# Sums by accumulating transfers, a deeper matrix scheme in two more chunks, and another bank in the last step of a normalised attention with four experts

## The chip, the cores and the metric

The kernel runs on one core of a Trainium2 chip. The metric is the device time of one execution, in microseconds (us). The kernel before took 1731.64 us, the median of three runs (1731.56 to 1731.66). The engines are TensorE (PE), VectorE (DVE), ScalarE (ACT), GpSimd (POOL) and SyncE (SP); PE writes to PSUM banks, and POOL and SP issue transfers. PEld in the profile is the weight load of TensorE.

## The reference

Attention without softmax over 8 batches, 8 heads, 576 positions and a head size of 64, then four experts on the 4608 tokens, each 512 to 1024 to 512 with a ReLU between, mixed by probabilities:

```python
kv = einsum('bhsd,bhse->bhde', k, v)
out = einsum('bhsd,bhde->bhse', q, kv)
x = out / sqrt(mean(out * out, axis=-1) + 1e-06) * g_norm      # then (B,H,S,D) -> (B*S, H*D)
p = domain_probs / (domain_probs.sum(-1, keepdims=True) + 1e-09)
for e in range(4):
    h = maximum(x @ w1[e], 0.0)
    out += p[:, e:e+1] * (h @ w2[e])
```

All is float32.

## The kernel before

The tokens are nine chunks of 512, so that experts and chunks make 36 steps, s = 9e + c, from 0 to 35. Each step has an up product (`x @ w1`) and a down product (`h @ w2`). Both are done by a Strassen-Winograd scheme, which replaces the eight products of a matrix in quarters by seven, at the price of more additions. The up product does it on two levels: seven outer products, and each of those made of seven inner ones.

```python
ORDER = (1, 6, 2, 5, 7, 4, 3)      # inner products, in this order
MERGED = (1, 6, 5, 7, 4, 3, 2)
OUTER = (1, 2, 6, 5, 3, 7, 4)      # outer products, in this order
BANKS = {"u1": 2, "u2": 2, "db": 2, "ab": 2}      # the eight PSUM banks
```

After each outer product m of the up product, whose 128 x 1024 result lies in a tile `made[m]` ("big"), the outer sums that have become possible are made. `add` is one tensor_tensor of 128 x 1024 on DVE or POOL, `relu` one activation of 128 x 1024 in place on ACT, `unit(f)` a new tile:

```python
for i, m in enumerate(OUTER):
    ...                      # 49 matmul groups in all; ACT and DVE empty the banks
    if m == 2:
        add(key, unit(1), made[1], made[2])
        relu(key, h[1])
    elif m == 6:
        add(key, made[1], made[1], made[6])
    elif m == 5:
        add(key, made[6], made[1], made[5])
    elif m == 3:
        add(key, unit(21), made[6], made[3])
        relu(key, h[21])
        add(key, unit(7), h[1], h[21], ALU.subtract)
    elif m == 7:
        ...                  # made[1] += made[7], then h[4], h[5], h[6]
    elif m == 4:
        add(key, unit(2), made[1], made[4])
        relu(key, h[2])
        add(key, unit(3), h[2], h[6], ALU.subtract)
```

The down product has two forms. `down` has one level: seven products for each of two halves of the tokens, each of four matmuls with 256 columns. `down_deep` has two levels: 49 products, each of two matmuls with 128 columns; it needs quarter sums of h and of w2, and outer sums of the results.

```python
def down(s, e, c):                            # one level
    for t in range(2):
        for j, m in enumerate(MERGED):
            kind = "ab" if e and t else "db"
            if m == 1:
                banks[1] = Buf(kind, f"d1_{s}_{t}")
            elif m in (2, 5):
                banks[2] = Buf(kind, f"d{m}_{s}_{t}")
            for kt in range(4):
                nc.tensor.matmul(ps[:, 0:256], ...)           # L1095
            ...                                               # weighted into acc: ACT or DVE
def down_deep(s, e, c):                       # two levels
    for i, group in enumerate(((1, 6), (7, 5), (4, 2), (3,))):
        ...                  # quarter sums of h: one add of 512 and two of 256 columns for each m
        for j, mm in enumerate(ORDER):
            for o, m in enumerate(group):
                for kt in range(2):
                    nc.tensor.matmul(ps[:, o * P:(o + 1) * P], ...)      # L1170
        ...                  # five copies on ACT and two sums on DVE for each group;
                             # seven outer sums of 128 x 512 in all (L1236), then weighted into acc

if e and c < NCH - 1:        # NCH is 9
    down_deep(s, e, c)
else:
    down(s, e, c)
```

So the nine steps of the first expert and the last step of each later expert (17, 26, 35) have the plain form. Results go to DRAM: in later experts by accumulating transfers that POOL issues, in the last step by plain stores of SP.

```python
if e and not again:          # again: s == 35
    nc.gpsimd.dma_start(out=dst, in_=cell(i)[parts, :], accum_op=ALU.add)      # L1065
else:
    nc.sync.dma_start(out=dst, in_=cell(i)[parts, :])                          # L1067
```

The order of all instructions on each engine is fixed ahead of the run by a list scheduler inside the kernel (`Plan.layout`). It simulates the engines with assumed durations, takes for each engine the most urgent operation that is ready, gives out buffers, and fixes what it took as that engine's order. For a transfer that POOL issues it assumes that it has landed 5.5 us after its issue, which takes 1.0 us:

```python
op.end = busy[eng] = t + op.cost[eng]
if op.kb:
    op.end += 5.5
```

On the chip each engine follows that order, and waits wherever an operand isn't there yet.

Of the kernel before, what the change touches and what calls it, by code (L numbers as in the profile page):

```python
# [10 lines left out]
ALU = mybir.AluOpType  # L11
# [219 lines left out]
def kernel(  # L231
# [36 lines left out]
    nc = tc.nc  # L268

    B, H, S, D = q.shape  # L270
    E, DM, F = moe_w1.shape
# [5 lines left out]
    NCH = B + 1  # L277
# [56 lines left out]
    plan = Plan()  # L334
# [4 lines left out]
    def dve(n):  # L339
        return {"DVE": 0.155 + 0.00104 * n}  # L340

    def act(n):
        return {"ACT": 0.155 + 0.00088 * n}
# [507 lines left out]
    def up(s, e, views):  # L851
        made = {}
        h = {}

        def add(key, to, a, b, op=ALU.add, where=either):
            combine(
                key, where(2 * NT), lambda: to.ap[:], lambda: a.ap[:], lambda: b.ap[:], op,
                [a, b], [to],
            )

        def relu(key, b):
            plan.add(
                key, act(2 * NT),
                lambda eng: nc.scalar.activation(out=b.ap[:], in_=b.ap[:], func=ACT.Relu),  # L864
                reads=[b], writes=[b],
            )

        for i, m in enumerate(OUTER):
            n = f"{s}_{m}"
            whole = made[m] = Buf("big", f"m{n}")  # L870
            bank = {
                1: Buf("u1", f"u1_{n}"), 2: Buf("u2", f"u2_{n}"), 5: Buf("u2", f"u3_{n}"),
            }
            snap = {}
            for j, mm in enumerate(ORDER):
                key = s + (i + j / 7) / 7
                ps = bank[{2: 2, 5: 5, 3: 5}.get(mm, 1)]

                def product(eng, m=m, mm=mm, ps=ps):
                    for u in range(2):  # L880
                        nc.tensor.matmul(  # L881
                            ps.ap[:, u * P:(u + 1) * P],
                            lhsT=w1f[e][m][mm][1]()[:, u * P:(u + 1) * P], rhs=views[m][mm][1](),
                            start=(mm in (1, 5) and u == 0), stop=True, skip_group_check=True,
                        )

                op = plan.add(
                    key, pe(2, P), product,
                    reads=w1f[e][m][mm][0] + [views[m][mm][0]] + ([ps] if mm == 2 else []),
                    **{"parts" if mm == 2 else "writes": [ps]},  # L890
                    after=last[-2:-1] if mm == 1 else seeds if mm == 5 else (),
                )
                op.marks, op.seed = (ps, HN), mm == 2
                if mm == 3:
                    last.append(op)

                def copy(to, where, ps=ps, key=key):
                    return plan.add(
                        key - 0.4, act(HN),
                        lambda eng: nc.scalar.activation(  # L900
                            out=where(), in_=ps.ap[:, 0:HN], func=ACT.Copy),
                        reads=[ps], parts=[to],
                    )

                def total(a, t, src, add_, whole=whole, key=key):
                    plan.add(
                        key - 0.4, dve(HN),
                        lambda eng: nc.vector.tensor_tensor(  # L908
                            out=block(whole, a, t), in0=src.ap[:, 0:HN], in1=add_.ap[:], op=ALU.add),
                        reads=[src, add_], parts=[whole],  # L910
                    )

                if mm == 1:
                    seeds = [copy(bank[2], lambda b=bank[2]: b.ap[:, 0:HN])]
                elif mm in (6, 7):
                    snap[mm] = Buf("snap", f"s{mm}_{n}")
                    copy(snap[mm], lambda b=snap[mm]: b.ap[:])
                if mm == 2:
                    copy(whole, lambda whole=whole: block(whole, 0, 0))
                elif mm == 7:  # L920
                    total(1, 1, bank[5], snap[7])
                elif mm == 4:
                    copy(whole, lambda whole=whole: block(whole, 1, 0))
                elif mm == 3:
                    total(0, 1, ps, snap[6])
            key = s + (i + 1) / 7

            def unit(f):
                h[f] = Buf("big", f"h{f}_{s}")
                return h[f]  # L930

            if m == 2:
                add(key, unit(1), made[1], made[2])
                relu(key, h[1])
            elif m == 6:
                add(key, made[1], made[1], made[6])
            elif m == 5:
                add(key, made[6], made[1], made[5])
            elif m == 3:
                add(key, unit(21), made[6], made[3])  # L940
# [3 lines that stand above are left out]
                add(key, made[1], made[1], made[7])  # L944
                add(key, unit(4), made[1], made[5], where=dve)
                relu(key, h[4])
                add(key, unit(5), h[21], h[4], where=dve)
                add(key, unit(6), h[5], h[1], ALU.subtract, dve)
            elif m == 4:
                add(key, unit(2), made[1], made[4])  # L950
                relu(key, h[2])
                add(key, unit(3), h[2], h[6], ALU.subtract)
        hidden[s] = h
# [123 lines left out]
    def down(s, e, c):  # L1077
        h = hidden.pop(s)
        base = s + 1.2
        merge, send = result(s, e, c, base)  # L1080
        second = []
        for t in range(2):
            banks = {}
            for j, m in enumerate(MERGED):
                key = base + (7 * t + j + 0.5) / 14
                kind = "ab" if e and t else "db"
                if m == 1:
                    banks[1] = Buf(kind, f"d1_{s}_{t}")
                elif m in (2, 5):
                    banks[2] = Buf(kind, f"d{m}_{s}_{t}")  # L1090
                ps = banks[1 if m in (1, 6, 7, 4) else 2]

                def product(eng, m=m, t=t, ps=ps):
                    for kt in range(4):
                        nc.tensor.matmul(  # L1095
                            ps.ap[:, 0:HN], lhsT=four(h[m])[:, kt // 2, t, kt % 2, :],
                            rhs=w2f[e][m].ap[:, kt * HN:(kt + 1) * HN],
                            start=(m in (1, 2, 5) and kt == 0), stop=(kt == 3),
                            skip_group_check=True,
                        )  # L1100

                op = plan.add(
                    key, pe(4, HN), product, reads=[h[m], w2f[e][m]], writes=[ps],
                    after=second[-1:] if t and m in (1, 5) else (),
                )
                op.marks = ps, HN
                if m == 2:
                    second.append(op)
                i, half, fresh = {
                    1: (t, 0, True), 2: (t, 0, False), 6: (t, 1, True), 3: (t, 1, False),  # L1110
                    5: (2 + t, 1, True), 7: (2 + t, 1, False), 4: (2 + t, 0, True),
                }[m]
                merge(key - 0.4, [ps], lambda ps=ps: ps.ap[:, 0:HN], i, half, fresh)
            send(base + 0.5 * (t + 1), t)
            send(base + 0.5 * (t + 1), 2 + t)
# [171 lines left out]
    for e in range(E):  # L1287
        for c in range(NCH):
            s = e * NCH + c
# [11 lines left out]
                up(s, e, x_views.pop(s))  # L1301
            if c == 0 and e:
                inner[e]()
            if e and c < NCH - 1:
                if not primed:
                    banks = [Buf("ab", f"prime{i}") for i in range(2)]

                    def prime(eng, banks=banks):
                        for b in banks:
                            nc.tensor.matmul(b.ap[:, 0:P], lhsT=ident[:], rhs=ident[:], start=True,  # L1310
                                             stop=False, skip_group_check=True)
                            nc.tensor.matmul(b.ap[:, P:HN], lhsT=ident[:], rhs=ident[:], start=False,
                                             stop=True, skip_group_check=True)

                    primed.append(plan.add(s + 1.1, pe(4, P), prime, writes=banks))
                    primed[0].marks = banks[0], HN
# [3 lines that stand above are left out]
# [7 lines left out]
    with tc.manual_schedule(engines={ENG.PE, ENG.DVE, ENG.Activation, ENG.Pool, ENG.SP}):  # L1327
# [4 lines left out]
        for op in order:  # L1332
# [6 lines left out]
            made = op.fn(op.eng)  # L1339
# [34 lines left out]
```

## Time and profile before

| What | Value |
|---|---|
| time | 1731.64 us |
| span of the profiled execution | 1729.4 us |
| busy: PE, PEld, DVE, ACT, POOL | 1719.6, 1652.0, 1222.8, 938.6, 616.5 us |
| matmul records | 15334 |
| HBM read and written | 145.30 and 73.14 MB |

One float32 matmul instruction leaves two matmul records in this trace: the plain down product has 12 steps of 56 matmuls, which is 672, and its groups have 1344 records together. The recorded ends of matmuls overlap, so the time of a matmul is read from the distance of the starts and not from the mean duration of a record. A group "L360" holds the adds of a helper, through which nearly all tensor_tensor operations of DVE and POOL go, so the shapes must be kept apart.

### The profile page before, as it was taken

The numbers are of one execution on the slowest core, as the hardware profiler recorded it, in microseconds if no ns is written. First come the engines' busy times: TensorE is split into PE (matmuls) and PEld (weight loads), VectorE is DVE, ScalarE is ACT, GpSimd is POOL, SyncE is SP. The second block draws the span as 40 slices with busy tenths as digits, with TensorE's granted clock in tenths as the row PEclk, the third lists the DMA queues.
The fourth block names the chain that finished last, engine by engine and source line by source line (L and its number), as shares of the span: only waits on it lengthen the run. The fifth ranks groups of instructions, "written<-read, shape, count | busy, mean of one in ns | idle before, by whom it ended". The sixth has DMA issues, their size and how long they took to land.

```text
span 1729.4 us, 38448 instructions
## 1 busy us (share of the span) xinstructions
PE 1719.6 (99%) x15334; PEld 1652.0 (96%) x15334; DVE 1222.8 (71%) x1968; ACT 938.6 (54%) x2300; POOL 616.5 (36%) x561
## 2 busy tenths in 40 slices
PE   9999999999999999999999999999999999999998
PEld 7699999999999999999999999999999999999997
DVE  4755655565676777777788877777788877777774
ACT  3354544454444565656555556566555556665652
POOL 3421323133334333333345333333345333333331
PEclk9999999999999999999999999999999999999999
DMA  9756444633333343534465344444475344444442
GB/s 240 218 161 193 153 122 131 193 135 128 147 130 99 94 114 104 116 106 113 131 185 110 99 110 111 111 111 110 114 204 110 98 111 111 110 110 109 112 99 49
DMA packets 148596, 220.94 MB, mean 128 GB/s; under 512 B 49600, under 2 KB 90816, under 8 KB 148416
## 3 DMA queue, kind: packets, MB, share of 16 engines
q1 hardware_dynamic: 133312, 191.21, 35.6%
q0 software_dynamic: 15104, 27.27, 11.0%
q8 instruction: 120, 1.97, 0.5%
q14 instruction: 60, 0.49, 0.1%
HBM read 145.30 MB, written 73.14 MB: 126 GB/s over the span
## 4 chain that ended last, share of the span: by engine, by line
PE 99%; POOL 0%; ACT 0%; DVE 0%; issue 0%; POOLq 0%
PE u L881 45%; PE db L1170 19%; PE db L1095 15%; PE ab L1170 12%; PE ab L1095 2%; PE u L968 2%; PE ab L634 1%; PE ab L678 1%; PE ab L620 1%; PE ab L1323 1%; PE ab L660 1%; PE db L660 0%; POOL rt L551 0%; PE ab L722 0%; PE ab L704 0%; PE ab L738 0%
## 5 line engine op out<-in xcount | busy, mean ns | idle before, releaser
L360 DVE TENSOR_TENSOR big<-big,big 128x1024 f32<-128x1024 f32 (+1 forms) x449 | 440.9, 995 | 34.9 <-ACT big L864 23.8
L881 PE MATMUL u<-xf,big 128*128 128x128 f32 x3104 | 453.3, 276 | 0.0
L881 PEld LDWEIGHTS u<-xf,big 128*128 128x128 f32 x3104 | 401.5, 192 | 2.2
L881 PE MATMUL u<-xf,w1y 128*128 128x128 f32 x2652 | 389.9, 276 | 0.0
L908 DVE TENSOR_TENSOR big<-u,snap 128x256 f32<-128x256 f32 x430 | 181.3, 422 | 235.9 <-PE u L881 176.4
L881 PEld LDWEIGHTS u<-xf,w1y 128*128 128x128 f32 x2652 | 343.6, 192 | 2.1
L900 ACT ACTIVATE snap<-u 128x256 f32<-128x256 f32 x490 | 187.7, 383 | 251.6 <-PE u L881 212.2
L1095 PE MATMUL db<-big,big 128*128 128x256 f32 x1136 | 269.0, 382 | 2.1 <-DVE big L560 2.1
L1095 PEld LDWEIGHTS db<-big,big 128*128 128x128 f32 x1136 | 207.1, 192 | 25.4 <-DVE big L560 2.3
L900 ACT ACTIVATE big<-u 128x256 f32<-128x256 f32 x430 | 164.7, 383 | 110.6 <-PE u L881 75.5
L360 POOL TENSOR_TENSOR big<-big,big 128x256 f32<-128x256 f32 (+1 forms) x139 | 172.5, 1248 | 132.3 <-DVE big L360 46.8
L1170 PE MATMUL db<-big,big 128*128 128x128 f32 x1056 | 146.9, 276 | 0.4 <-ACT snap L1198 0.4
L864 ACT ACTIVATE big<-big 128x1024 f32<-128x1024 f32 x128 | 134.5, 1051 | 3.4 <-POOL big L360 2.1
L1170 PEld LDWEIGHTS db<-big,big 128*128 128x128 f32 x1056 | 132.1, 192 | 0.6 <-ACT snap L1198 0.6
L1236 POOL TENSOR_TENSOR big<-big 128x512 f32<-128x512 f32 x26 | 33.0, 1268 | 269.2 <-DVE big L360 263.9
L1198 ACT ACTIVATE snap<-db 128x256 f32<-128x256 f32 x192 | 68.4, 356 | 100.0 <-PE db L1170 95.1
L360 POOL TENSOR_TENSOR big<-big 128x512 f32<-128x512 f32 (+1 forms) x57 | 70.3, 1232 | 126.8 <-DVE big L360 102.6
L1170 PE MATMUL db<-kv,big 128*128 128x128 f32 x804 | 114.7, 275 | 0.0
L1065 POOL DMA_DIRECT2D out_dram<-big x100 | 91.2, 987 | 47.4 <-ACT snap L1198 22.8
L900 ACT ACTIVATE u<-u 128x256 f32<-128x256 f32 x245 | 90.9, 371 | 28.1 <-PE u L881 8.0
L1170 PEld LDWEIGHTS db<-kv,big 128*128 128x128 f32 x804 | 102.1, 192 | 0.1
L1206 DVE TENSOR_TENSOR big<-ab,snap 128x256 f32<-128x256 f32 x140 | 59.1, 422 | 57.4 <-ACT snap L1198 31.9
(213 smaller groups left out, 2676.9 us busy)
## 6 DMA issues: line engine op xcount, KB each, us to landing
xf<-x SPq DMA_DIRECT2D x108, 512.0 KB, 3.6
out_dram<-big POOLq DMA_DIRECT2D x84, 256.0 KB, 5.8
xf<-x_h SPq DMA_DIRECT2D x81, 256.0 KB, 3.2
xf<-x SPq DMA_DIRECT2D x81, 256.0 KB, 3.3
x<-xf SPq DMA_DIRECT2D x36, 512.0 KB, 6.1
big<-in_moe_w_dram SPq DMA_DIRECT2D x25, 512.0 KB, 4.8
small<-in_q_dram SPq DMA_DIRECT2D x72, 128.0 KB, 4.8
kv<-in_k_dram SPq DMA_DIRECT2D x30, 288.0 KB, 4.8
```

Source lines behind the costliest of these rows:

```text
L360: lambda eng: adder(eng).tensor_tensor(out=out_(), in0=a(), in1=b(), op=op),
L864: lambda eng: nc.scalar.activation(out=b.ap[:], in_=b.ap[:], func=ACT.Relu),
L881: nc.tensor.matmul(ps.ap[:, u * P:(u + 1) * P], lhsT=w1f[e][m][mm][1]()[:, u * P:(u + 1) * P], rhs=views[m][mm][1](), start=(mm in (1, 5) ...
L900: lambda eng: nc.scalar.activation(out=where(), in_=ps.ap[:, 0:HN], func=ACT.Copy),
L908: lambda eng: nc.vector.tensor_tensor(out=block(whole, a, t), in0=src.ap[:, 0:HN], in1=add_.ap[:], op=ALU.add),
L968: nc.tensor.matmul(bank.ap[:], lhsT=two(w.ap[:])[:, kt, ut * P:(ut + 1) * P], rhs=two(xh[dh].ap[:])[:, kt, :], start=(dh == kt == 0), stop ...
L1065: nc.gpsimd.dma_start(out=dst, in_=cell(i)[parts, :], accum_op=ALU.add)
L1095: nc.tensor.matmul(ps.ap[:, 0:HN], lhsT=four(h[m])[:, kt // 2, t, kt % 2, :], rhs=w2f[e][m].ap[:, kt * HN:(kt + 1) * HN], start=(m in (1, ...
L1170: nc.tensor.matmul(ps.ap[:, o * P:(o + 1) * P], lhsT=b.ap[:, col:col + P], rhs=w2q[e][m][mm][1]()[:, kt, :], start=(mm in (1, 5) and o == ...
L1198: lambda eng: nc.scalar.activation(out=where(), in_=group_of(ps.ap), func=ACT.Copy),
L1206: lambda eng: nc.vector.tensor_tensor(out=cell(tq, dq), in0=group_of(src.ap), in1=group_of(add_.ap), op=ALU.add,),
L1236: lambda eng: adder(eng).tensor_tensor(out=whole(to), in0=whole(a), in1=whole(b), op=ALU.add),
```

## The change

It has three parts. In steps 9 to 33, three of the outer sums of each up product are no longer made by DVE or POOL, but by a transfer within SBUF which adds its source onto its destination. POOL issues it (one instruction, 128 rows of 4096 bytes). That frees the arithmetic engines, and spares the new tile of the sum, as the sum lies where an operand lay. Second, the down products of steps 17 and 26 take the two-level form, so that the plain form is left to the first expert and step 35. Third, in step 35 the bank of products 2, 3, 5 is taken from "u2", which the up products no longer need there, in place of "db" and "ab".

```diff
+        by_dma = e > 0 and s < 34
+
+        def accumulate(key, to, a):
+            plan.add(
+                key, {"POOL": 1.0},
+                lambda eng: nc.gpsimd.dma_start(out=to.ap[:], in_=a.ap[:], accum_op=ALU.add),
+                reads=[a, to], writes=[to], kb=512,
+            )
...
-            if m == 2:
+            if m == 2 and by_dma:
+                h[1] = made[2]
+                accumulate(key, h[1], made[1])
+                relu(key, h[1])
+            elif m == 2:
                 add(key, unit(1), made[1], made[2])
                 relu(key, h[1])
+            elif m == 6 and by_dma:
+                accumulate(key, made[6], made[1])
+                made[1] = made[6]
+                made[6] = None
             elif m == 6:
                 add(key, made[1], made[1], made[6])
             elif m == 5:
+                made[6] = made[6] or Buf("big", f"v{s}")
                 add(key, made[6], made[1], made[5])
...
             elif m == 4:
-                add(key, unit(2), made[1], made[4])
+                if by_dma:
+                    h[2] = made[4]
+                    accumulate(key, h[2], made[1])
+                else:
+                    add(key, unit(2), made[1], made[4])
                 relu(key, h[2])
                 add(key, unit(3), h[2], h[6], ALU.subtract)
...
                 elif m in (2, 5):
-                    banks[2] = Buf(kind, f"d{m}_{s}_{t}")
+                    banks[2] = Buf("u2" if s == E * NCH - 1 else kind, f"d{m}_{s}_{t}")
...
-            if e and c < NCH - 1:
+            if e and s < E * NCH - 1:
```

## The prediction

> **What bounds the kernel.** I read first the busy times and the slices of the page, then the engines by stretches of the span, then what PE waited for, and last the timeline, to get the pace of each kind of matmul.
>
> ```profile
> PE 1719.6 (99%) x15334; PEld 1652.0 (96%) x15334; DVE 1222.8 (71%) x1968; ACT 938.6 (54%) x2300; POOL 616.5 (36%) x561
> ...
> 0.00:72.00 72.00, 67.97 (x754) 47.22 (x754) 42.53 (x84) 25.36 (x62) 27.28 (x29) 1.00 0.93 248
> 72.00:520.00 448.00, 447.13 (x4205) 412.27 (x4206) 267.62 (x484) 219.02 (x502) 131.10 (x101) 1.00 0.46 149
> ...
> 560.00:900.00 340.00, 340.00 (x3047) 340.00 (x3046) 258.88 (x394) 203.25 (x513) 127.27 (x115) 1.00 0.47 121
> 900.00:960.00 60.00, 60.00 (x435) 57.16 (x434) 50.14 (x79) 32.55 (x78) 32.81 (x36) 1.00 0.50 114
> ...
> 1700.00:1729.40 29.40, 24.82 (x114) 21.18 (x113) 9.15 (x18) 3.62 (x8) 5.81 (x5) 0.98 0.43 72
> ```
>
> After each stretch and its length come the busy times of PE, PEld, DVE, ACT and POOL with their counts, the granted clock, the share of the DMA engines and GB/s. From 560 to 900 us, the deep steps of the second expert, PE has no idle time, and 3047 records in 340 us are one every 111.6 ns. The same count comes out of 960 to 1300 us. A pace that regular, with weight loads filling the same time, says that PE is at its own limit and not waiting inside its busy time. PE's whole idle time is 1729.4 - 1719.6 = 9.8 us: 4.0 in the first 72 us, 0.9 up to 520, 0.4 shortly before 1700, and 4.6 at the end.
>
> ```profile
> PE db L1095 <- DVE big L560: 2.1, 1, 2.1
> PE ab L1323 <- POOL ident masks.py:199: 1.4, 1, 1.4
> PE u L881 <- ACT snap L900: 0.6, 1, 0.6
> ```
>
> The three largest of six entries of what PE waited for (total, times, longest) belong to the start; a single further one of 0.4 us, on an ACT copy, lies just before 1700 us. No wait recurs, so nothing that makes DVE, ACT or POOL faster can shorten the span by itself. Only fewer or cheaper matmuls can, or the 4.6 us of the end.
>
> The pace of the two forms, from the timeline (start, duration, records at the end of the line):
>
> ```profile
> 1666.36 0.61 PE L881 MATMUL u<-xf,big 128*128 128x128 f32 x4
> 1666.81 0.61 PE L881 MATMUL u<-xf,w1y 128*128 128x128 f32 x4
> 1667.26 0.61 PE L1170 MATMUL db<-kv,big 128*128 128x128 f32 x4
> ...
> 1712.57 8.80 PE L1095 MATMUL ab<-big,big 128*128 128x256 f32 x40
> 1721.21 1.89 PE L1095 MATMUL ab<-small,big 128*128 128x256 f32 x8
> ```
>
> Four records of 128 columns take 0.45 us from start to start; I use the 111.6 ns of the stretch. Forty of 256 columns take 1721.21 - 1712.57 = 8.64 us, 216 ns each.
>
> **What the Trainium skill says.** "Perfetto Trace Analysis", section "Identifying the Most-Contended Engine", says that matmul busy share is a poor measure of the distance to PE's limit and that the busy share of weight loads is a good one. The trace agrees: PEld is busy 340.00 of 340.00 us. "DMA: Bandwidth & Descriptors", section "SWDGE vs HWDGE vs iDMA", says that a transfer that accumulates must be issued by GpSimd, and that transfers of all issuing engines run on the same 16 DMA engines. Here the accumulating stores are POOL's, as said. "SBUF — State Buffer", section "Who interferes with whom", says that DMA has ports of its own and doesn't slow compute engines down; nothing in this trace tests that for a transfer within SBUF. The page on DMA, section "Anatomy of one DMA", fits a transfer from GpSimd by 2.0 us plus bytes over 436 GB/s. That would make 3.2 us of 512 KB. The measured accumulating store of 256 KB takes 5.8, so I don't use the fit.
>
> **Second level in steps 17 and 26.** It removes 2 x 56 matmuls of 256 columns, 224 records: 224 x 0.216 = 48.4 us. It adds 2 x 98 of 128 columns, 392 records: 392 x 0.1116 = 43.7 us. The order of the changed kernel confirms the count: 7968 matmuls against 7884, and 84 is 2 x (98 - 56). All of it is on the path, as PE is. The sum is **-4.6 us**. What the deep form adds elsewhere is off the path as long as it keeps up: for each step DVE or POOL do 7 quarter sums of 512 and 14 of 256 columns, 8 bank sums and 7 outer sums. With 1.01 us (the 512 of L360), 0.52 (the 256), 0.42 (the bank sum) and 0.72 (L1236) that is 7.1 + 7.3 + 3.4 + 5.0 = 22.8 us, less six weighted sums of 0.48, so about +20 us a step; ACT gets 20 more copies of 0.36, 7 us.
>
> **Three sums by transfers.** 25 steps times three are 75 adds of 128 x 1024 gone, and 75 issues on POOL in their place.
>
> ```profile
> L360 DVE TENSOR_TENSOR big<-big,big 128x1024 f32<-128x1024 f32 x263 | 348.7, 1330 | 33.8 <-ACT big L864 23.8 <-DMA big<-in_moe_w_dram 1.2 <-PE u L881 0.3
> L360 POOL TENSOR_TENSOR big<-big,big 128x1024 f32<-128x1024 f32 x43 | 101.6, 2363 | 52.5 <-DVE big L908 12.0 <-DVE big L1049 11.9 <-DVE big L360 10.2
> L1065 POOL DMA_DIRECT2D out_dram<-big x100 | 91.2, 987 | 47.4 <-ACT snap L1198 22.8
> ...
> out_dram<-big POOLq DMA_DIRECT2D x84, 256.0 KB, 5.8
> xf<-x SPq DMA_DIRECT2D x108, 512.0 KB, 3.6
> ```
>
> In the first three lines the numbers after the bar are busy us, mean ns and idle before. By the order, 72 of the 128 x 1024 operations leave DVE (355 to 283) and 3 leave POOL (66 to 63). DVE loses 72 x 1.33 = 96 us and gains most of 2 x 20 from the second level: about 1165 us busy. POOL gains 75 x 0.95 = 71 us for the issues. Neither is PE, so the direct gain is **0 us**. What it buys is room: from 900 to 960 us, where a new expert's weights are formed, DVE was busy for 50.1 of 60 us, and a second level there asks for more.
>
> What it can cost is a wait. Two of the three sums go straight to a ReLU on ACT, and ACT works in order: if the transfer is late, the copies that empty PE's banks stand behind the ReLU. So I compare when the transfer lands with where its reader stands. By order, I counted the matmuls that PE has between the issue and its first reader and multiplied by PE's pace. For the 50 ReLUs that is 6.9 to 9.8 us, median 7.6; for 22 adds on POOL 6.2 to 10.3, median 6.7; for 3 adds on DVE 14 us or more. Landing, from the last two lines: 256 KB accumulated take 5.8 us. Its packets of 2048 bytes take 178 ns in the median, about twice the 84 of a plain packet of that size; a plain packet of 4096 takes 159, so an accumulating one should take some 335. Eight rows a DMA engine make 2.7 us of 512 KB against 1.4 of 256: 1.3 more, so an estimated 7.1 us. That leaves 0.5 us of slack at the median ReLU, and none where stores of a previous result are issued one or two us ahead on the same queue, which the order shows at about half the first sums. I choose: 15 of 50 ReLUs late by 1 us, and PE loses a third of that, as it has two banks of each kind: 5 us; the POOL adds cost nothing. Because landing within SBUF spares the way to HBM, I halve it: **+2.4 us**, with a wide error.
>
> **Another bank in the last step.** Before, the plain products of step 35 stood together after the last deep ones, with PE idle for 0.4 us just ahead. By order they now stand among them. After PE's last product there remain one weighted sum and the last store in either kernel, so the 4.6 us of the end stay. I give it **-0.4 us**.
>
> **The sum.** 1731.6 - 4.6 + 2.4 - 0.4 = 1729.0 us; as all errors but one are in one direction, I put the middle at 1728.8.
>
> **The rivals.** (1) All transfers land in time: only PE's work counts, and the time is about 1726.7. For it speak the slack at the median and ACT's idle share of 46%. Against it, no transfer within SBUF has been seen here. (2) Late transfers hold ACT regularly: 50 ReLUs late by 1 to 2 us, half of it passed on to PE, is 25 to 50 us, and the time becomes 1752 to 1777. For it speaks that the planner's 5.5 us after issue, which fit a 256 KB store, are used for twice the size. Against it: most readers stand further off than that. (3) DVE becomes the bound around the changes of expert: 20 us more in a stretch with 10 us idle in 60, less two or three adds a step by transfer (4 us). If POOL, idle for 27 of those 60 us, doesn't take it up, 2 to 5 us at each of two places return, and the gain is gone: 1731 to 1736. (4) The DMA engines get full: 75 x 128 packets of 335 ns over 16 engines are 201 us, 12% of the span on top of a share of 0.47. The loads of x that take 3.6 us would take longer, but stand several buffers ahead; I expect nothing on PE.
>
> **Range and chances.** The floor is -5.0 us, so the low end is 1726.3. The upper end takes half of the mildest form of rival 2: 1738. Faster by over 2% (below 1697) has nothing to come from: 0.01. Slower by over 2% needs +35 us, rival 2 in full: 0.03. Within 2%: 0.96. That it is faster at all I hold for about 70% likely.
>
> **What would show it.** L1095 must have 224 records fewer, L1170 392 more, with PE idle still near 10 us if rival 1 holds. What PE waited for tells rivals 2 and 3 apart: entries on ACT copies of line 900 or 1198 that recur, with ACT itself waiting for a DMA at the ReLU, mean late transfers; the same entries with ACT waiting for DVE, only near 900 and 1300 us, mean DVE. The landing of the new transfers should be 6 to 8 us; below 6 my cost is too high, above 8 far too low. Wrong altogether is the argument if the pace of deep steps leaves 111.6 ns without any wait on record, as then the transfers disturb PE's reads.

## The result, and the profile after

The changed kernel takes 1744.45 us (median of four runs, 1742.59 to 1745.48) against 1731.6: ratio 1.0074, 95% interval 1.0056 to 1.0091. It is 12.8 us slower, where the prediction had 2.8 us faster and a range up to 1738.

Busy times and records on the page of the changed kernel:

```profile
PE 1721.8 (99%) x15502; PEld 1655.9 (95%) x15502; DVE 1151.2 (66%) x1961; ACT 947.2 (54%) x2340; POOL 667.8 (38%) x628
```

The 168 more matmul records are the predicted 392 less 224. DVE lost 72 us net. PE's idle time has grown from 9.8 to 1743.7 - 1721.8 = 21.9 us. That is not all PE lost: the recorded ends of matmuls overlap the next start, so a short stop leaves no idle time. The number of records in a stretch shows it all. The same stretches of the two kernels (first before, then after; columns as in the prediction):

```profile
560.00:870.00 310.00, 310.00 (x2779) 310.00 (x2778) 232.60 (x357) 187.93 (x474) 112.83 (x103) 1.00 0.44 113
970.00:1270.00 300.00, 300.00 (x2689) 300.00 (x2688) 229.57 (x349) 182.53 (x461) 107.09 (x101) 1.00 0.45 114
```

```profile
560.00:870.00 310.00, 307.08 (x2733) 305.68 (x2733) 202.27 (x335) 182.71 (x462) 118.68 (x114) 1.00 0.61 145
870.00:970.00 100.00, 98.56 (x877) 97.96 (x876) 80.27 (x142) 58.55 (x153) 45.82 (x47) 1.00 0.68 168
970.00:1270.00 300.00, 297.60 (x2647) 296.17 (x2646) 205.57 (x335) 179.06 (x453) 132.83 (x131) 1.00 0.63 148
1270.00:1370.00 100.00, 98.18 (x874) 97.57 (x873) 81.17 (x142) 57.31 (x149) 45.62 (x46) 1.00 0.67 168
```

In the deep steps away from the changes of expert, 46 and 42 records are missing: 88 x 0.1116 = 9.8 us, and DVE is less busy there than before. From 1370 to 1680 us another 51 are missing, and around the changes of expert 19 and 22 of the 896 that the pace makes of 100 us: 180 records or 20.1 us in all. So the loss is spread over all steps with transfers, and away from the changes of expert a lack of time on DVE is not behind it. What PE waited for, and then who waited for the new transfers (line 867; us, times), in the changed kernel:

```profile
PE u L891 <- ACT snap L910: 8.9, 12, 1.2
PE u L891 <- DVE big L918: 1.8, 2, 1.0
```

```profile
  ACT big L874: 25.0, 16
  POOL big L360: 8.7, 6
  DVE big L360: 5.6, 2
  ACT small L874: 3.1, 2
...
DMA to landing us min/median/max: 4.5/7.2/10.6
```

The view counts the landing from the start of the issue. The planner's 5.5 us count from the end of the issue, which it takes to last 1.0 us, so on the scale of the view it planned with 6.5, which is less than the median of 7.2.

ACT's bank copies of line 910 now recur as what PE waits for, and 18 ReLUs (line 874) waited 28.1 us for a transfer; before, no ReLU had one to wait for. One such case in the timelines of ACT and then PE (start, duration, and in brackets the idle time before):

```profile
620.66 1.06 ACT L874 ACTIVATE big<-big 128x1024 f32<-128x1024 f32 x1 [2.21 <-DMA big<-big]
621.62 0.36 ACT L910 ACTIVATE snap<-u 128x256 f32<-128x256 f32 x1
```

```profile
620.57 0.61 PE L1193 MATMUL ab<-big,small 128*128 128x128 f32 x4
622.04 0.71 PE L891 MATMUL u<-xf,big 128*128 128x128 f32 x4 [0.86 <-ACT snap L910]
622.83 1.16 PE L891 MATMUL u<-xf,w1y 128*128 128x128 f32 x8
623.82 0.61 PE L1193 MATMUL ab<-x_rem,big 128*128 128x128 f32 x4
```

ACT stood 2.21 us before the ReLU, and the bank copies behind it came late. PE started its next product 1.47 us after the last instead of 0.45: 1.0 us lost, of which the view calls 0.86 idle. The next starts come late as well: the 16 records from 620.57 to 623.82 take 3.25 us, where the pace makes 1.79, so some 1.5 us are lost in all.

Worked in this way from the starts of PE's records around each of the 18 late ReLUs, PE lost 15.4 us of their 28.1: each time the wait less 0.6 to 0.9 us, which is at most 0.25 us at the six waits below 1 us. Another 4.3 us went at four other waits: two adds on DVE that waited 2.6 and 3.0 us for a new transfer (0.9 and 1.3 us of PE), an add on DVE that waited 3.1 us for a load of weights (1.1), and a copy on ACT that waited 2.9 us for a store (1.1). Around the waits of POOL for the transfers, 8.7 us in six cases, PE's records keep their pace.

### The profile page after: what moved, and what is told of

It is laid out like the page before. It is cut to its first block, busy times and chain, and to the rows that moved or that the text cites. A ratio compares the mean times of both kernels' runs of the same rounds, so it can differ in the third digit from the quotient of the medians.

```text
span 1743.7 us, 39108 instructions
## 1 busy us (share of the span) xinstructions
PE 1721.8 (99%) x15502; PEld 1655.9 (95%) x15502; DVE 1151.2 (66%) x1961; ACT 947.2 (54%) x2340; POOL 667.8 (38%) x628
## 4 chain that ended last, share of the span: by engine, by line
PE 89%; DMA 7%; POOL 1%; ACT 1%; issue 1%; DVE 1%; POOLq 0%; ACTq 0%; DVEq 0%
PE u L891 40%; PE db L1193 17%; PE db L1118 13%; PE ab L1193 10%; DMA big<-big 5%; PE u L991 2%; PE ab L634 1%; DMA big<-small 1%; PE ab L1346 1%; PE ab L620 1%; PE ab L678 1%; PE ab L660 1%; POOL out_dram L1088 1%; PE u L1118 1%; DMA out_dram<-big 1%
## 5 line engine op out<-in xcount | busy, mean ns | idle before, releaser
L891 PE MATMUL u<-xf,big 128*128 128x128 f32 x3392 | 491.7, 276 | 8.4 <-ACT snap L910 8.4
L891 PEld LDWEIGHTS u<-xf,big 128*128 128x128 f32 x3392 | 435.3, 192 | 12.7 <-ACT snap L910 10.7
L360 DVE TENSOR_TENSOR big<-big,big 128x1024 f32<-128x1024 f32 (+1 forms) x391 | 380.0, 983 | 46.9 <-ACT big L874 26.6
L1118 PE MATMUL db<-big,big 128*128 128x256 f32 x1040 | 246.0, 380 | 2.1 <-DVE big L560 2.1
L1118 PEld LDWEIGHTS db<-big,big 128*128 128x128 f32 x1040 | 188.4, 191 | 22.3 <-DVE big L560 2.3
L1193 PE MATMUL db<-big,big 128*128 128x128 f32 x1088 | 154.2, 276 | 0.0
L1193 PEld LDWEIGHTS db<-big,big 128*128 128x128 f32 x1088 | 137.5, 192 | 0.3
L1221 ACT ACTIVATE snap<-db 128x256 f32<-128x256 f32 x208 | 74.0, 356 | 109.6 <-PE db L1193 108.6
L1193 PE MATMUL db<-kv,big 128*128 128x128 f32 x840 | 121.1, 276 | 0.8 <-ACT snap L1221 0.8
L360 DVE TENSOR_TENSOR big<-big 128x512 f32<-128x512 f32 (+1 forms) x111 | 85.6, 774 | 47.2 <-ACT big L874 45.8
L1193 PEld LDWEIGHTS db<-kv,big 128*128 128x128 f32 x840 | 107.2, 192 | 1.0 <-ACT snap L1221 1.0
```

The lines of the kernel that those rows point to most:

```text
L360: lambda eng: adder(eng).tensor_tensor(out=out_(), in0=a(), in1=b(), op=op),
L891: nc.tensor.matmul(ps.ap[:, u * P:(u + 1) * P], lhsT=w1f[e][m][mm][1]()[:, u * P:(u + 1) * P], rhs=views[m][mm][1](), start=(mm in (1, 5) ...
L1118: nc.tensor.matmul(ps.ap[:, 0:HN], lhsT=four(h[m])[:, kt // 2, t, kt % 2, :], rhs=w2f[e][m].ap[:, kt * HN:(kt + 1) * HN], start=(m in (1, ...
L1193: nc.tensor.matmul(ps.ap[:, o * P:(o + 1) * P], lhsT=b.ap[:, col:col + P], rhs=w2q[e][m][mm][1]()[:, kt, :], start=(mm in (1, 5) and o == ...
L1221: lambda eng: nc.scalar.activation(out=where(), in_=group_of(ps.ap), func=ACT.Copy),
```

## The experiments

Theory A: transfers that land later than the planner assumed hold ACT at the ReLUs, and ACT holds PE. The rivals: B, DVE is the bound where the deep form meets the forming of weights; C, the new order of the matmuls; D, the traffic or the issues of the transfers as such. Ratios are to the kernel before, with 95% intervals.

| Run | us | Ratio | Interval |
|---|---|---|---|
| changed kernel | 1744.45 | 1.0074 | 1.0056 to 1.0091 |
| e1_no_acc | 1732.74 | 1.0008 | 1.0000 to 1.0017 |
| e2_acc_only | 1751.37 | 1.0121 | 1.0104 to 1.0138 |
| e3_plan_9 | 1728.83 | 0.9988 | 0.9981 to 0.9995 |
| e4_short (sums left out) | 1726.10 | 0.9970 | 0.9959 to 0.9981 |
| e5_bank_only | 1730.64 | 0.9996 | 0.9988 to 1.0004 |
| e6_m6_only | 1730.65 | 0.9997 | 0.9989 to 1.0005 |
| e7_relu_only | 1749.30 | 1.0104 | 1.0087 to 1.0121 |
| e8_plan_9_8 | 1727.19 | 0.9976 | 0.9967 to 0.9986 |
| e9_near | 1735.55 | 1.0026 | 1.0015 to 1.0037 |
| e10_plan_7 | 1727.27 | 0.9978 | 0.9970 to 0.9986 |
| e11_near4 | 1727.14 | 0.9976 | 0.9966 to 0.9985 |
| e12_half (sums left out) | 1727.76 | 0.9980 | 0.9972 to 0.9987 |
| e13_no_acc_8 | 1733.07 | 1.0011 | 1.0004 to 1.0018 |
| e14_near4_55 | 1729.29 | 0.9989 | 0.9982 to 0.9995 |

### e1_no_acc: without the transfers

```diff
-        by_dma = e > 0 and s < 34
+        by_dma = False
```

> The changed kernel with its 75 sums made by DVE and POOL again, the second level in steps 17 and 26 and the bank of the last step kept. Theory A (late transfers hold ACT at the ReLUs, and PE behind it, for some 17 us): the whole loss goes with the transfers, and PE's work alone counts, 1731.6 - 4.6 - 0.4 = 1726.6, within 1 us; PE waits for ACT copies no longer recur. Theory B (the loss lies where DVE has to take the deep form beside the weights of the next expert): the loss stays or grows, 1736 or more, as DVE now has the adds as well. Theory C (the new order of the matmuls as such costs time): above 1731.

Measured 1732.74 us. The large loss went with the transfers; that it isn't the matmul order either, the unchanged order of e4_short below shows. But it isn't 1726.6: 6.6 us above the run with short transfers below. Two of its stretches:

```profile
870.00:970.00 100.00, 99.12 (x883) 98.58 (x882) 85.35 (x145) 57.68 (x150) 44.36 (x43) 1.00 0.49 130
1270.00:1370.00 100.00, 97.51 (x862) 96.42 (x862) 88.71 (x146) 55.77 (x143) 42.87 (x42) 1.00 0.45 124
```

```profile
PE u L891 <- DVE big L918: 2.6, 3, 1.0
```

Around the two changes of expert, 13 and 34 of 896 records are missing (896 is the run of e4_short), 47 x 0.1116 = 5.2 us of the 7.2 us between the two profiled executions. DVE is busy for 85 and 89 of 100 us there (83 in e4_short), and PE waits for sums of DVE (line 918). So B is right as well, as e11_near4 and e13_no_acc_8 below confirm, for a smaller loss that the changed kernel's transfers were made to avoid. Neither theory foresaw both.

### e2_acc_only: the transfers alone

```diff
-            if e and s < E * NCH - 1:
+            if e and c < NCH - 1:
-                    banks[2] = Buf("u2" if s == E * NCH - 1 else kind, f"d{m}_{s}_{t}")
+                    banks[2] = Buf(kind, f"d{m}_{s}_{t}")
```

> The kernel before with the 75 transfers alone; steps 17 and 26 in the plain form, the old banks in the last step. Theory A: the loss of some 17 us is all here, without the 4.6 us of saved matmuls: 1746 to 1750. Theory B: no loss without the deep form in steps 17 and 26, 1731.6 within 1 us.

Measured 1751.37 us, a little beyond its range and 20.0 us above the 1731.35 of its comparison. The loss needs neither the second level nor the bank.

### e3_plan_9: the planner told of a later landing

```diff
-                            op.end += 5.5
+                            op.end += 9.0 if op.kb == 512 else 5.5
```

> The changed kernel, with the planner told that an accumulating transfer of 512 KB lands 9.0 us after its issue instead of 5.5, so that by order most ReLUs stand 9.4 to 12.5 us of matmul work behind their issue (median 10.9) instead of 6.9 to 9.8 (median 7.6). The transfers themselves and their number are the same. Theory A: the transfers now land ahead of their readers, ACT no longer waits for a DMA, and the time falls to 1727 to 1729. Theory D (what costs time is the transfers' traffic or the issue on POOL itself): little changes, 1742 or more.

Measured 1728.83 us. The 75 transfers and their bytes are the same, only their readers stand later in the order. The group of the ReLUs (busy us, mean ns, idle before), first in the changed kernel, then here:

```profile
L874 ACT ACTIVATE big<-big 128x1024 f32<-128x1024 f32 x123 | 129.4, 1052 | 26.3 <-DMA big<-big 20.0 <-DMA big<-small 5.0 <-DVE big L360 1.1
```

```profile
L874 ACT ACTIVATE big<-big 128x1024 f32<-128x1024 f32 x129 | 135.6, 1051 | 1.9 <-DVE big L360 1.6 <-DMA big<-big 0.2
```

25.0 us of waiting for transfers became 0.2, and 15.6 us of time went with them. This is theory A, and against D. One wait of PE of 1.8 us was left at 1331 us, on a DVE operation that itself stood 3.8 us for an accumulating store to let its tile go.

### e4_short: the same order, shorter transfers

```diff
-                lambda eng: nc.gpsimd.dma_start(out=to.ap[:], in_=a.ap[:], accum_op=ALU.add),
+                lambda eng: nc.gpsimd.dma_start(out=to.ap[:, 0:128], in_=a.ap[:, 0:128], accum_op=ALU.add),
```

> The changed kernel with each of the 75 transfers cut to the first 128 of 1024 columns: seven eighths of each sum are left out. The order of all engines is the same, instruction for instruction, as is the number of issues. A transfer should land in 4 to 5 us instead of 7.2. Theory A: the waits of ACT vanish with the landing time, 1726.5 to 1728. Theory C or the issue on POOL: unchanged at 1742 to 1746.

Measured 1726.10 us, 0.4 us below its range, with seven eighths of each of the 75 sums left out; landing in 4.5 us in the median. Every engine has the order of the changed kernel, and POOL its issues. So neither order nor issues cost the 18.3 us, but how long the transfers take. It is also the floor: its PE rate is full in all stretches.

```profile
560.00:870.00 310.00, 310.00 (x2779) 310.00 (x2778) 206.27 (x343) 187.75 (x474) 121.97 (x119) 1.00 0.47 117
870.00:970.00 100.00, 100.00 (x896) 99.90 (x896) 83.17 (x147) 59.05 (x152) 48.03 (x51) 1.00 0.55 141
```

### e12_half: bytes or landing

```diff
-                lambda eng: nc.gpsimd.dma_start(out=to.ap[:], in_=a.ap[:], accum_op=ALU.add),
+                lambda eng: nc.gpsimd.dma_start(out=to.ap[:, 0:512], in_=a.ap[:, 0:512], accum_op=ALU.add),
```

> The changed kernel, order and issues unchanged, with each of the 75 transfers cut to 512 of 1024 columns: half of each sum is left out. A transfer of 256 KB should land in 5.5 to 6 us in the median. Theory A: the loss follows the landing: of the 18 us between short (1726.1) and whole (1744) transfers a few are left, 1727 to 1732. Rival (the loss is a matter of bytes moved, not of when they land): half of it, about 1735.

Measured 1727.76 us, with half of each sum left out; landing in 5.3 us (3.3 to 9.2), a little sooner than expected. Half the bytes leave 1.7 of 18.3 us of loss, so it doesn't go by bytes. Who waited for the transfers:

```profile
  ACT big L874: 8.9, 11
...
  ACT small L874: 0.6, 1
DMA to landing us min/median/max: 3.3/5.3/9.2
```

Twelve ReLUs still waited, 9.5 us in all, 0.8 us each, and PE lost 2.0 us around them, a fifth; in the changed kernel 28.1 us of 1.56 each cost 15.4, over half. One rule covers both runs, which have the same order: PE loses the wait less 0.6 to 1.0 us. So a short wait of ACT is absorbed, and of a long one all but this slack is passed on.

### e6_m6_only and e7_relu_only: which readers

```diff
 e6_m6_only
-            if m == 2 and by_dma:
+            if False:
...
-                if by_dma:
+                if False:
                     h[2] = made[4]
 e7_relu_only
-            elif m == 6 and by_dma:
+            elif False:
```

> The changed kernel with only one of the three sums by transfer, the one after product 6, whose readers are adds on POOL (18) and DVE (7) that stand as near as 5.8 us; the two sums ahead of a ReLU are made by DVE or POOL again. Theory A (only the ReLUs on ACT pass the lateness on): ACT doesn't wait for a DMA, nothing is lost to the transfers, and as DVE is relieved by 25 of 75 adds the time lies between the 1726.1 of the short transfers and the 1732.7 without any: 1728 to 1732. Rival (a late operand on POOL costs PE as well): 1735 or more.

> The changed kernel with the transfers for the two sums ahead of a ReLU alone (50 of 75); the sum after product 6 is made by DVE or POOL. The planner has its 5.5 us, and the ReLUs stand 6.0 to 9.8 us of matmul work (median 7.6) behind their issue, as in the changed kernel. Theory A (the ReLUs on ACT carry the loss): ACT waits for transfers at a third of the ReLUs and the time stays near the changed kernel's, 1738 to 1748. Rival (the reader of the third sum on POOL carries it): 1728 to 1732.

Measured 1730.65 and 1749.30 us, the latter a little beyond its range. In the first, POOL waited long for transfers:

```profile
POOL big L360 <- DMA small<-big: 38.9, 7, 7.1
POOL big L360 <- DMA big<-big: 5.1, 1, 5.1
POOL big L360 <- DMA big<-small: 5.0, 1, 5.0
```

With these 49 us of waiting on POOL the kernel is 2.1 us faster than without transfers, and around each of these waits PE's records keep their pace. ACT did wait for the transfers, against the expectation: 7.3 us in five cases, at copies of line 910, and PE lost nothing there. In the second, ReLUs waited 36.2 us in 23 cases, and PE lost 15.6 us around them. POOL stood there for transfers as well, 81.6 us in 12 cases, so that this run alone doesn't tell the two readers apart; together with the first it does, as waits of POOL cost PE nothing there. So the transfers ahead of ACT carry most of the loss. The profiled execution of e7_relu_only lies 23.7 us above that of e4_short, and most of what the ReLUs don't explain stands around the two changes of expert, as in e1_no_acc.

### e10_plan_7 and e8_plan_9_8: how much later is enough

```diff
 e10_plan_7
-                            op.end += 5.5
+                            op.end += 7.0 if op.kb == 512 else 5.5
 e8_plan_9_8
-                            op.end += 5.5
+                            op.end += 9.0 if op.kb == 512 else 8.0
```

> The changed kernel with the planner at 7.0 us after issue: the ReLUs stand 7.8 to 10.7 us of matmul work behind their issue, median 9.2. With landings of 4.5 to 10.6 us, median 7.2, most transfers are now in time and a few aren't. Theory A: between the 1744 of 5.5 us and the 1728.8 of 9.0, nearer to the latter: 1729 to 1733. Rival (the 9.0 us plan is faster by a lucky order): no such place between.

> As the run with the planner at 9.0 us, with accumulating stores of 256 KB planned at 8.0 us after issue as well, because the one wait of PE left there (1.8 us at 1331 us) hangs on a DVE operation that waited 3.8 us for such a store to let go of its tile. Theory A: that wait goes, and the time comes to within 1 us of the short transfers, 1726 to 1727.5, clear of both kernels. Rival (traffic of whole transfers costs time in itself): stays at 1728.8.

Measured 1727.27 and 1727.19 us. The first is below its range: 1.5 us more in the plan removed nearly the whole loss (three ReLUs waited, 1.2 us in all). The second shows no wait of PE after the first 80 us. Both are faster than either kernel, clear of noise. With whole transfers and this plan the kernel is 1.1 us above the run with short ones.

### e9_near, e11_near4, e13_no_acc_8 and e14_near4_55: where the room is needed

```diff
 e9_near: as e8_plan_9_8, and
-        by_dma = e > 0 and s < 34
+        by_dma = s in (16, 17, 18, 25, 26, 27)
 e11_near4: as e8_plan_9_8, and
+        by_dma = s in (17, 18, 26, 27)
 e13_no_acc_8: as e1_no_acc, and
-                            op.end += 5.5
+                            op.end += 8.0
 e14_near4_55: as e11_near4, with
+                            op.end += 9.0 if op.kb == 512 else 5.5
```

> The same, with transfers only in the six steps around the two changes of expert (16, 17, 18, 25, 26, 27), 18 transfers instead of 75. If the room on DVE is needed only where the deep form meets the forming of weights (there the kernel without transfers lost 5.2 of its 7.2 us against the short ones), the time is that of the run with all transfers, 1726 to 1728. If DVE is short of time in all deep steps, it is 1730 or more.

> As the run with transfers in six steps around the changes of expert, in four of them (17, 18, 26, 27), 12 transfers. There a load of weights took 11.4 us to land beside other transfers at 872 us, and PE then stood for 3.9 us. If that was one collision of transfers and the room on DVE is needed near the changes only, this comes to 1727 to 1730. If the few transfers don't suffice, 1731 to 1733 as without any; if a load is late again, about 1735.

> The kernel without transfers within SBUF, its accumulating stores planned at 8.0 us after issue instead of 5.5. If DVE is the bound around the changes of expert, it stays near 1732.7 (1731 to 1734). If the stores' late landing was the cause there, it falls to 1727 to 1728.

> Twelve transfers in steps 17, 18, 26 and 27 planned at 9.0 us, the stores at 5.5 as before. If the twelve transfers are the cure, 1727 to 1729, as with the stores at 8.0. If the stores' planning was, 1731 to 1733.

Measured 1735.55, 1727.14, 1733.07 and 1729.29 us, the last 0.3 us above its range. e9_near missed: a load of weights took 11.4 us to land, DVE stood 5.5 us for it, and PE 3.9 us for DVE. The landings of such loads from 840 to 900 us, the two waits, and two stretches of this run:

```profile
DMA to landing us min/median/max: 3.4/4.4/11.4
...
DVE big L360 <- DMA big<-in_moe_w_dram: 6.9, 2, 5.5
...
PE u L891 <- DVE big L918: 3.9, 1, 3.9
...
870.00:890.00 20.00, 16.10 (x128) 15.91 (x127) 12.10 (x20) 8.04 (x20) 6.43 (x7) 0.89 0.82 213
890.00:910.00 20.00, 20.00 (x171) 20.00 (x170) 14.05 (x30) 8.39 (x24) 7.02 (x7) 0.94 0.63 179
```

PE's stand cost more than its 3.9 us. After it the granted clock, the third number from the end, is 0.89 and 0.94 in the two stretches, which costs another 20 x 0.11 + 20 x 0.06 = 3.4 us. Together that is 7.3 us, which accounts for the 66 records that are missing from 870 to 970 us (830 of 896, 7.4 us). The transfers from 870 to 886 us, with the busy share of the DMA engines in 40 slices in tenths, and some of the issues:

```profile
DMA  9999999999969789999999999999958996210000
...
xf<-x SPq DMA_DIRECT2D x1, 512.0 KB, 8.1
big<-big POOLq DMA_DIRECT2D x1, 512.0 KB, 10.6
```

The engines are all but full for 13 us, and what is issued early in this stretch lands late: the load of x in 8.1 us against a median of 3.6 in the kernel before. D is thus true at one place in one order, but not the general loss. With transfers in four steps the collision is absent: 12 of 75 transfers do all the good of 75. The later plan for the stores alone does nothing (1733.07); the twelve transfers alone bring it to 1729.29; both to 1727.14. The fastest complete versions, e11_near4, e8_plan_9_8 and e10_plan_7, can't be told apart.

### e5_bank_only: the bank alone

```diff
-                    banks[2] = Buf(kind, f"d{m}_{s}_{t}")
+                    banks[2] = Buf("u2" if s == E * NCH - 1 else kind, f"d{m}_{s}_{t}")
```

> The kernel before with the bank of the last step alone changed. The prediction's step: 0.4 us less, as the plain products of step 35 mix with the last deep ones and PE's gap of 0.4 us goes: 1731.0 to 1731.4. Rival: the order of the two last steps was bound by something else, and it changes nothing, or it adds a gap.

Measured 1730.64 us, below its range, against 1731.26 for the kernel before. PE's wait of 0.4 us before the last step is gone from the trace, but the interval includes 1: not shown, and at most some 2 us.

## Why the prediction was wrong

- **What bounds the kernel**: right. Whatever sped up the kernel did it by keeping PE's pace at 111.6 ns a record.
- **The second level, -4.6 us**: right. With the bank the floor of -5.0 was predicted, and e4_short lies 5.25 us below before; the records changed by +168 as counted. The shares of the two parts in this are not told apart.
- **The landing, 7.1 us**: right, 7.2 in the median. A 4096-byte accumulating packet took 328 ns in the median, where 335 was worked out.
- **The cost of late transfers, +2.4 us**: this step failed, and its mechanism was right. It was 18.3 us, by e4_short. Of its factors, 15 late ReLUs were 18; 1 us each was 1.56; a third passed on to PE was over half (15.4 of 28.1); and the final halving, because transfers within SBUF spare the way to HBM, had no measurement behind it: the landing that it shortened was the one just estimated. The product without the halving, 5 us, would still have been under a third. The step set a median landing against a median distance, where the spread (4.5 to 10.6 against 6.9 to 9.8) decides how late a transfer is; and it took the passed-on share as a constant, where PE lost each wait less 0.6 to 1.0 us, and so most of a long one. It also left out that adds on DVE would wait for transfers (5.6 us in two cases, of which PE lost 2.1); it held the three readers on DVE to be 14 us or more away, and whether these two adds are among them isn't shown.
- **"The POOL adds cost nothing"**: right; in e6_m6_only and in the changed kernel PE keeps its pace around POOL's waits.
- **Room on DVE, rival 3**: right about the kernel without transfers, which lies 6.6 us above e4_short, in the main around the two changes of expert. The direct gain of the transfers is therefore not 0 beside the second level, but what makes its 4.6 us come through.
- **The bank, -0.4 us**: not decided.
- **Rival 2**: it won, with 18.3 us, less than its stated 25 to 50, and by the sign that was named for it: PE waits on ACT copies, and ACT on a DMA at the ReLU. The range left it almost no place. Its ends also don't fit the sums beside them: the floor of -5.0 us makes 1726.6 and not 1726.3, and half of 25 us on top of that makes 1739 and not 1738; neither slip decides anything here.
- **Rival 4, full DMA engines**: small in the changed kernel, where the one load of weights that DVE waited 3.1 us for cost PE 1.1 us; e9_near shows that a collision of transfers can cost 7.4.

## What to carry to other kernels

An order that is fixed ahead needs assumed durations well above the median of what a transfer takes, above all before an engine that works in a fixed order and also empties PSUM: here 1.5 us more in one constant, which had fitted a transfer of half the size, was worth 17 us. To price a late operand, take the spread of the landing and not its median, ask what stands behind the waiting operation on its engine, and take off the slack that it has: here 0.6 to 1.0 us, beyond which the whole wait reached PE. Relieve an engine that isn't the bound only where it runs short: 12 transfers did what 75 did.

## What the runs showed of the hardware

- Landing by size of accumulating transfers within SBUF, in the same order: 64 KB 4.5 us, 256 KB 5.3, 512 KB 7.2 in the median, with 10.6 at the most. The fit in "DMA: Bandwidth & Descriptors" of the Trainium skill, section "Anatomy of one DMA", from which an estimate of 3.2 us for 512 KB follows, is far too low here; the section says nothing of accumulating transfers.
- With the later plans, the same 512 KB landed in 6.3 to 6.4 us in the median (e3_plan_9, e8_plan_9_8, e10_plan_7) instead of 7.2, and in 6.2 with fewer of them (e6_m6_only, e7_relu_only); the reason stays open.
- After PE had stood for 3.9 us in e9_near, the granted clock was 0.89 and 0.94 in the next two stretches of 20 us and 1.00 after them. After a stand of 1.8 us, in e3_plan_9, it stayed at 1.00.
